# Other ranks and times in the list that orders a fused attention, Fourier mixing and feed-forward kernel

## The chip, the core and the metric

One core of a Trainium2 chip runs the whole program. It has a matrix engine (TensorE, PE), three engines for elementwise work (VectorE or DVE, ScalarE or ACT, GpSimd or POOL) and a synchronising engine (SyncE, SP), which issues most transfers. Each engine executes its own list of instructions in order, and waits on semaphores for the others. The metric is the device time of one execution in microseconds; the lower the better.

## What is computed

Attention with a causal window over 8 batches, 8 heads and 576 positions of 64 features (half of the heads look at every fourth position), then a layer that mixes tokens by the real part of a two-dimensional Fourier transform, normalises, and applies a feed-forward product with 512 by 2048 by 512 weights. All in float32; the weights come as 64-bit floats, which the kernel converts on the chip.

```
scores = where(mask, q @ k.T / 8, -1e9); attn = softmax(scores); x = attn @ v    # (8, 576, 512)
u  = x + real(fft(fft(x, axis=1), axis=2))
un = (u - mean(u)) / sqrt(var(u) + 1e-6)
out = u + relu(un @ w_ch1) @ w_ch2
```

## The kernel before

**An order by rank.** No instruction is written in its final place. Every step is entered with `add(engine, cost, fn, reads, writes, prio)`; then `Plan.run` walks through an imagined time with the entered costs. Whenever an engine is free, it takes of the steps whose inputs are ready the one with the smallest `prio`. The order that comes out is the program's; each engine then runs it in order on the chip, whatever the true durations are. So a number in the table of ranks (`P_...`) can move instructions all over the program.

**Early stage, to about 600 us.** For each batch b, `attention(b)` works on 4 pairs of heads, each in three units of two blocks: score products (L581, bank `sc`), a masked maximum on VectorE (L589, it needs `mask_sb`), exponentials on ScalarE (L595), transposes on TensorE (L608), products with the values (L615) and a normalisation (L627); results go to DRAM. `mix(b)` reads them, folds them (L760), transforms along the sequence (L797) and the channels (L843), and normalises. The 2048 hidden features are 16 blocks of 128. Six of them are *resident*: `prep_w` converts their 64-bit weights once (L922 to L941, twelve conversions into `wa1` and `wa2`). `fill(ut, tiles)` runs these six blocks for two tiles of 128 tokens: `up` (L1021, 72 matmuls per two tiles, corrected on VectorE at L1029) and then `down` (L1037, 36 matmuls, the second products), and `keep_part` stores the two part sums.

**Handover.** Meanwhile `blocks` converts the other ten blocks (tile `wst`, stored in DRAM as `wt`). When the transform is done, `left_w` takes its place in SBUF; when the conversions are done, `late_w` takes the staging buffers' place, and the last weights go into the seats of the resident ones (`places`).

**Late stage.** Ten hidden blocks are five pairs, worked off for nine chunks of 512 tokens by a scheme of seven block products in place of eight. `load_blocks(c)` reads a chunk's rows (L1132, four transfers), transposes them on VectorE (L1142), forms four differences (L1192) and fills `xb` (casts at L1202, corrections at L1205). `two_tiles(p)` issues seven up products (L1351, all into one PSUM bank, `ff`, in groups of 6 or 12 matmuls); after each group `snap` copies the bank out on ScalarE (L1359) before the next one may write it; sums and operands follow on VectorE (L1387, L1376, L1380). `down7` issues the second products (L1459). `prepare` fetches the tokens' rows and part sums, `finish` writes the output. The ranks here are `SOON + 0.001 * clock` for elementwise work and `LAST + 0.01 * clock` for matmuls, where `clock` counts the second products issued so far; up products are ahead by `P_UP`.

## Time and profile before

| | |
|---|---|
| median of 3 runs | 1074.49 us (1071.9 to 1077.31) |
| profiled execution | 1072.93 us, span 1071.2 us |
| TensorE busy / its weight loads | 1031.3 us (96%) / 964.0 us (90%) |
| VectorE busy | 888.1 us (83%) |
| ScalarE busy | 623.9 us (58%) |
| GpSimd busy | 221.0 us (21%) |
| moved by transfers | 158.19 MB, 148 GB/s over the span |
| chain that ended last | PE 77%, DVE 12%, DMA 6% |

Busy shares are averages over stages with different limits. Ends of matmuls are modelled, so the busy time of TensorE is no measure of its peak. The granted clock tells which of TensorE's two levels holds: 1.00 is 2.4 GHz, 0.50 is 1.2 GHz. The profiled execution is 1.56 us below the median of the three runs, and 1.7 us longer than its span.

### The profile page before, as it was taken

What the parts mean: (1) busy time and instruction counts of PE and PEld (TensorE: products, weight loads), DVE (VectorE), ACT (ScalarE), POOL (GpSimd) and SP (SyncE); (2) the same over time, 40 slices, a digit from 0 to 9 for tenths busy, and PEclk for the clock granted to TensorE, in tenths of its full rate; (3) what the DMA queues carried; (4) which work ended last, traced back from release to release, by engine and by line L of the source; (5) the groups of instructions that cost most, each with busy time, mean ns of one, the idle gap of its engine ahead of it and who ended that gap; (6) DMA issues with size and microseconds to landing.
All of it is one profiled execution on the core that took longest, in us unless ns stands there. A gap on an engine that the chain in (4) does not pass through costs nothing.

```text
span 1071.2 us, 22723 instructions
## 1 busy us (share of the span) xinstructions
PE 1031.3 (96%) x7876; PEld 964.0 (90%) x7876; DVE 888.1 (83%) x2847; ACT 623.9 (58%) x1588; POOL 221.0 (21%) x278
## 2 busy tenths in 40 slices
PE   4899999999999999999999899999999999999996
PEld 3778898888899899999899799999999999999996
DVE  4898996987888956669988568989998989989886
ACT  3798775865745232345445356666665757565753
POOL 1021524364463545400000000201010000110020
PEclk9899999999999999999999899999999999999999
DMA  8968855865545325254778952333323242332131
GB/s 271 284 208 260 241 167 160 228 200 161 181 126 161 95 86 147 69 168 138 238 254 255 332 199 40 99 63 106 82 87 85 76 110 66 102 80 89 31 103 57
DMA packets 116451, 158.19 MB, mean 148 GB/s; under 512 B 11032, under 2 KB 64472, under 8 KB 116336
## 3 DMA queue, kind: packets, MB, share of 16 engines
q1 hardware_dynamic: 112752, 148.03, 47.5%
q0 software_dynamic: 3040, 8.09, 2.5%
q8 instruction: 62, 1.02, 0.4%
q10 hardware_dynamic: 544, 0.62, 0.2%
q14 instruction: 53, 0.43, 0.1%
HBM read 108.40 MB, written 48.29 MB: 146 GB/s over the span
## 4 chain that ended last, share of the span: by engine, by line
PE 77%; DVE 12%; DMA 6%; issue 2%; ACT 1%; SPq 1%; DVEq 0%; ACTq 0%
PE ff L1351 19%; PE ff L1021 9%; PE ff L1037 8%; PE sc L581 7%; PE sc L1459 5%; PE mix L1459 5%; PE av L615 4%; PE mix L843 3%; PE pt L1459 3%; PE av L1459 3%; PE ff L1459 3%; PE mix L797 2%; DMA ut<-us 2%; PE pt L608 2%; DVE ut L1142 2%
## 5 line engine op out<-in xcount | busy, mean ns | idle before, releaser
L595 ACT ACTIVATE pm<-pm,mx 96x128 f32<-96x128 f32 x384 | 129.2, 394 | 37.2 <-DVE mx L589 35.3
L1076 POOL DMA_INDIRECT ut<-us,flip_sb x20 | 36.3, 1816 | 536.2 <-DMA wa<-wt 132.0
L1021 PE MATMUL ff<-ut,wa 128*128 128x256 f32 x936 | 125.6, 285 | 2.4 <-DVE h L1029 2.4
L581 PE MATMUL sc<-kb,tq 128*96 128x256 f32 x384 | 109.6, 403 | 15.1 <-issue 9.9
L1021 PEld LDWEIGHTS ff<-ut,wa 128*128 128x128 f32 x936 | 116.4, 188 | 4.6 <-DVE h L1029 2.8
L589 DVE CUSTOM_DVE_ANT_0 pm<-sc,mask_sb 96x128 f32<-96x128 f32 x384 | 91.6, 279 | 26.9 <-DMA mask_sb<-in_mask_dram 9.3
L1037 PE MATMUL ff<-wa,h 128*128 128x512 f32 x468 | 113.9, 394 | 0.0
L1037 PEld LDWEIGHTS ff<-wa,h 128*128 128x128 f32 x468 | 85.9, 188 | 16.6
L1142 DVE STREAM_TRANSPOSE ut<-ut 128x512 f32<-128x512 f32 (+1 forms) x76 | 73.0, 988 | 14.4 <-DMA ut<-us 14.2
L581 PEld LDWEIGHTS sc<-kb,tq 128*96 128x96 f32 x384 | 57.6, 173 | 29.2 <-issue 15.5
L615 PEld LDWEIGHTS av<-vt,ptsb 128*96 128x96 f32 x672 | 68.8, 167 | 12.1 <-DVE xt L627 3.2
L1351 PE MATMUL ff<-xb,wa 128*128 128x256 f32 x540 | 76.4, 281 | 0.8 <-ACT s L1359 0.6
L615 PE MATMUL av<-vt,ptsb 128*96 128x65 f32 x672 | 71.9, 249 | 5.3 <-DVE xt L627 4.1
L1351 PEld LDWEIGHTS ff<-xb,wa 128*128 128x128 f32 x540 | 68.4, 188 | 2.2 <-ACT s L1359 1.0
L1351 PE MATMUL ff<-xb,left_w 128*128 128x256 f32 x486 | 68.1, 281 | 0.8 <-ACT s L1359 0.5
L1351 PE MATMUL ff<-xb,late_w 128*128 128x256 f32 x486 | 68.3, 279 | 0.0
L1373 ACT ACTIVATE h<-s 128x256 fp32r<-128x256 f32 x136 | 55.1, 415 | 13.7 <-DVE s L1389 8.9
L1351 PEld LDWEIGHTS ff<-xb,left_w 128*128 128x128 f32 x486 | 61.7, 188 | 1.5 <-ACT s L1359 0.9
L1351 PEld LDWEIGHTS ff<-xb,late_w 128*128 128x128 f32 x486 | 61.8, 188 | 0.4 <-ACT ut L1359 0.2
L1027 ACT ACTIVATE h<-ff 128x256 fp32r<-128x256 f32 x78 | 30.0, 384 | 54.2 <-PE ff L1021 53.8
L1351 PE MATMUL ff<-xb,right_w 128*128 128x256 f32 x378 | 53.4, 286 | 5.1 <-ACT ut L1359 3.2
L1029 DVE SCALAR_TENSOR_TENSOR h<-ff,h 128x256 fp32r<-128x256 f32 x78 | 32.6, 418 | 26.5 <-ACT h L1027 25.9
(247 smaller groups left out, 2593.0 us busy)
## 6 DMA issues: line engine op xcount, KB each, us to landing
vt<-in_v_dram SPq DMA_DIRECT2D x32, 390.0 KB
wst<-in_w_dram SPq DMA_DIRECT2D x20, 512.0 KB
wt<-wst SPq DMA_DIRECT2D x40, 256.0 KB
us<-uc SPq DMA_DIRECT2D x36, 257.0 KB
part<-row SPq DMA_DIRECT2D x36, 256.0 KB
ut<-us SPq DMA_DIRECT2D x36, 256.0 KB
ut<-part SPq DMA_DIRECT2D x36, 256.0 KB
kb<-in_k_dram SPq DMA_DIRECT2D x62, 144.0 KB
```

The lines of the kernel that those rows point to most:

```text
L581: nc.tensor.matmul(sc()[:QB, 256 * n:256 * n + 256], lhsT=tq()[:, cols], rhs=kb()[:, :, keys], start=True, stop=True,)
L589: nc.vector.tensor_tensor_reduce(pm()[:, i], sc()[:QB, KB * i:KB * i + KB], mask_sb()[:, masks[blocks[i // 2]]], -0.125, 3.0e38, ALU.add, ...
L595: add("ACT", 0.295, lambda i=i: nc.scalar.activation(out=pm()[:, i], in_=pm()[:, i], func=AF.Exp, bias=mx()[:, i:i + 1], scale=-1.0), ((mx ...
L615: add("PE", 0.17, lambda i=i: nc.tensor.matmul(av()[:QB, 65 * i:65 * i + 65], lhsT=pt()[:, i], rhs=vt()[:, i % 2, blocks[i // 2]], start=T ...
L1021: nc.tensor.matmul(z()[:, :n_tok], lhsT=wf()[:, a, kk], rhs=ut()[:, p, kk], start=(kk == 0 and n == 0), stop=(kk == KT - 1 and n == 2),)
L1029: add("DVE", dve(n_tok), lambda: nc.vector.scalar_tensor_tensor(h()[:, 1, :n_tok], z()[:, :n_tok], 0.0, h()[:, 0, :n_tok].bitcast(F32), op ...
L1037: nc.tensor.matmul(acc(), lhsT=h()[:, a, P * s:P * s + P], rhs=wf()[:, p], start=(first and n == 0), stop=(last and n == 2),)
L1076: add("POOL", 1.3, lambda: nc.gpsimd.indirect_dma_start(u(0, C + 2), None, us[idx // 4](), bass.IndirectOffsetOnAxis(ap=flip_sb()[:, 4 * k ...
L1142: nc.vector.transpose(out=o[back], in_=x[:, g])
L1351: nc.tensor.matmul(up_bank()[:, lo:lo + TOK1], lhsT=ap()[:, a, kk], rhs=xb()[:, j, p, kk], start=(start and k == 0), stop=(k == 5), skip_g ...
L1373: add("ACT", act(TOK1), lambda: nc.scalar.activation(out=ap()[:, 0], in_=src(), func=AF.Relu if relu else AF.Copy), need, (k0,), prio)
L1459: nc.tensor.matmul(acc()[:, TOK1 * half:TOK1 * half + TOK1], lhsT=ap()[:, a, P * half:P * half + P], rhs=wap()[:, q_].rearrange("p k f -> ...
```

## The change

It does four things. *Ranks*: the table of priorities has other numbers for attention, folds, fills, late loads and preparations; up products get `P_UP` 10.35 in place of 0.2, which ranks them ahead of all second products; small additions per batch and per conversion (`P_WS`, `P_MS`, `P_SS`) are new. *Last fill*: the second products of the last two resident tiles get their own rank, `LAST + P_BR`, and alternate between two banks. *Second chunk*: its rows and the preparations of the first chunk wait for a mark, which is set when the first pair's last operand is there. *First transfers*: mask, identity and permutation tables and the first values get ranks of -7 to -7.9, and the first queries and keys -7.8 in place of -25.06. Seats of the last weights go to all of `wa1` first, then to `wa2`. Some assumed costs of transfers on SP changed too.

```diff
-P_OP, P_GA, P_LB, P_FI = 0.0, 53.71, -74.28, 47.3
-P_PR = 91.31
-P_UP = 0.2
+P_OP, P_GA, P_LB, P_FI = 2.43, 48.72, -40.68, 47.3
+P_PR = 128.43
+P_UP = 10.35
+P_WS = [10, 11, 11, 10, 10, 10]
+P_SS = [10, 10, 10, 10, 15, 12, 10, 10]
+P_BR = -0.125
+LB_AT, PR_AT = 0, 0
...
-P_QK0, P_V0 = -25.06, -7.0
+P_QK0, P_V0 = -7.8, -7.0
...
-T_SEQ, T_CHN, T_STEP, P_SEQ, P_CHN = 7.07, 23.47, 3.91, -21.94, -1.92
+T_SEQ, T_CHN, T_STEP, P_SEQ, P_CHN = 10.36, 24.62, 1.0, -4.0, -2.0
...
-P_MASK, P_ID, P_PERM = -7.35, -14.41, 8.87
+P_MASK, P_ID, P_PERM = -7.9, -7.8, -7.0
...
-    def prepare(idx, seat, prio):
+    def prepare(idx, seat, prio, mark):
...
+        add("NONE", 0.0, lambda: None, (marks[mark],) if mark[0] == 0 else (), (uk,), prio)
...
-        add("NONE", 0.0, lambda: raw(), (), (raw,), prio)
+        add("NONE", 0.0, lambda: raw(), (marks[0, LB_AT],) if c == 1 else (), (raw,), prio)
...
+        if tiles[-1] == NTILE - 1:
+            accs = [bank("sc") for _ in tiles]
+            for f in range(NF1):
+                for s, acc in enumerate(accs):
+                    down(hs[f], wa2[f], acc, s, f == 0, f == NF1 - 1, LAST + P_BR)
+            for idx, acc in zip(tiles, accs):
+                keep_part(idx, acc, prio)
+            return
...
-        prep_w(f, wa1[f], wa2[f], utb, (), P_W + P_WF * f)
+        prep_w(f, wa1[f], wa2[f], utb, (), P_W + P_WF * f + P_WS[f] - 10)
...
-    places += [(x, i) for f in range(NF1) for x in (wa1[f], wa2[f]) for i in range(2)]
+    places += [(x, i) for wa in (wa1, wa2) for x in wa for i in range(2)]
...
             got = two_tiles(p)
+            marks[c, p] = Buf(ap=0)
+            add("NONE", 0.0, lambda: None, got[2][0], (marks[c, p],), SOON)
```

How the order moves is shown at three places. Line numbers of the changed file are higher, by 5 up to the resident fills, by 14 in the late stage. First, SP's list from the first transfers of the program, as far as the first values (`vt`). Before, from the second pair's keys on (the first pair's keys and queries stand ahead):

```order
L553 DMA kb1_175<-in_k_dram 64x576 x2
L556 DMA tq_255<-in_q_dram 128x576
L553 DMA kb2_176<-in_k_dram 64x576 x2
L556 DMA tq_266<-in_q_dram 128x576
L493 DMA ident_sb_163<-in_ident_dram 128x384
L492 DMA mask_sb_162<-in_mask_dram 96x384
L558 DMA vt_275<-in_v_dram 128x780
```

In the changed program the list begins with the mask (the queries and keys of the first pair come in thirds):

```order
L497 DMA mask_sb_162<-in_mask_dram 96x384
L498 DMA ident_sb_163<-in_ident_dram 128x384
L561 DMA tq_230<-in_q_dram 128x192
L558 DMA kb0_174<-in_k_dram 64x192 x2
L561 DMA tq_230<-in_q_dram 128x192
L558 DMA kb0_174<-in_k_dram 64x192 x2
L561 DMA tq_230<-in_q_dram 128x192
L499 DMA perm_sb_164<-in_perm_dram 96x288
L563 DMA vt_260<-in_v_dram 128x780
L558 DMA kb1_175<-in_k_dram 64x576 x2
```

The mask moved from behind all three pairs' queries and keys to the front, and the first values from behind them to between the first and the second pair. Second, TensorE's list at the handover; `ut` holds the last tiles' tokens, `h` their hidden values, `xb` the first late chunk. Before:

```order
L1037 MATMUL sc_8664<-wa2_2_158,h_8574 128x512 x3
L1037 MATMUL sc_8664<-wa2_3_159,h_8598 128x512 x3
L1037 MATMUL sc_8664<-wa2_4_160,h_8617 128x512 x3
L1037 MATMUL sc_8664<-wa2_5_161,h_8648 128x512 x3
L1351 MATMUL ff_8692<-xb_7169,right_w_5404 128x256 x36
L1459 MATMUL sc_8761<-right_w_5404,h_8743 128x256 x6
L1351 MATMUL ff_8692<-xb_7169,right_w_5404 128x256 x6
L1459 MATMUL av_8789<-left_w_7167,h_8779 128x256 x4
```

In the changed program:

```order
L1026 MATMUL av_8612<-ut_8252,wa1_5_155 128x256 x12
L1365 MATMUL ff_8638<-xb_7153,right_w_5449 128x256 x6
L1042 MATMUL sc_8649<-wa2_0_156,h_8526 128x512 x3
L1042 MATMUL sc_8587<-wa2_1_157,h_8544 128x512 x3
L1365 MATMUL ff_8638<-xb_7153,right_w_5449 128x256 x12
L1042 MATMUL sc_8649<-wa2_1_157,h_8544 128x512 x3
L1042 MATMUL sc_8587<-wa2_2_158,h_8573 128x512 x3
L1365 MATMUL ff_8638<-xb_7153,right_w_5449 128x256 x12
L1042 MATMUL sc_8649<-wa2_2_158,h_8573 128x512 x3
L1042 MATMUL sc_8587<-wa2_3_159,h_8592 128x512 x3
L1365 MATMUL ff_8638<-xb_7153,right_w_5449 128x256 x6
```

The first 36 matmuls of the up products stood in a row behind all second products of the last fill; now they begin directly behind its up products, and six second products stand between each two groups. Third, VectorE's list at the same place, from the correction of the fill's last hidden block (L1029, L1034). Before:

```order
L1029 SCALAR_TENSOR_TENSOR h<-av,h 128x256
L1142 STREAM_TRANSPOSE ut<-ut 128x4x4x32 x4
L1192 TENSOR_TENSOR ut<-ut 128x512 x3
L1387 TENSOR_TENSOR ut<-ut,ys 128x256
L1192 TENSOR_TENSOR ut<-ut 128x512
L1082 SCALAR_TENSOR_TENSOR ut<-ut 128x512
L1376 SCALAR_TENSOR_TENSOR h<-ut,h 128x256
```

In the changed program:

```order
L1034 SCALAR_TENSOR_TENSOR h<-av,h 128x256
L1401 TENSOR_TENSOR ut<-ut,ys 128x256
L1390 SCALAR_TENSOR_TENSOR h<-ut,h 128x256
L1401 TENSOR_TENSOR sb<-sb 128x256
L1403 SCALAR_TENSOR_TENSOR sb<-ut,sb 128x256
L1401 TENSOR_TENSOR s_8728<-s_8728,ut 128x256
```

The second chunk's transposes and differences are gone from here; the first of the transposes follows 31 rows behind the first sum.

## Rows read from the trace of the kernel before

**Rows 1.** Busy time by stage: us of PE, PEld, DVE, ACT, POOL; clock; DMA share; GB/s.

```profile
core 0: us, PE busy (x) PEld busy (x) DVE busy (x) ACT busy (x) POOL busy (x), PEclk, DMA share, GB/s
0.00:25.00 25.00, 11.12 (x47) 7.72 (x48) 9.79 (x73) 7.12 (x20) 3.52 (x10) 1.00 0.89 272
25.00:150.00 125.00, 117.95 (x906) 100.44 (x905) 115.72 (x633) 100.92 (x292) 33.82 (x46) 0.96 0.79 236
150.00:350.00 200.00, 197.41 (x1503) 176.39 (x1502) 163.21 (x766) 121.65 (x341) 91.87 (x127) 1.00 0.61 173
350.00:595.00 245.00, 243.91 (x1612) 223.80 (x1613) 192.95 (x452) 102.36 (x248) 55.49 (x76) 1.00 0.54 167
595.00:625.00 30.00, 24.91 (x157) 22.82 (x156) 16.53 (x32) 12.46 (x28) 2.04 (x2) 0.89 1.08 346
625.00:1050.00 425.00, 423.43 (x3557) 420.52 (x3556) 375.65 (x864) 273.96 (x649) 34.30 (x18) 1.00 0.31 82
```

**Rows 2.** Timeline of the start, all engines: start us, us, instruction, idle before it.

```profile
3.73 3.70 PE L581 MATMUL sc<-kb,tq 128*96 128x256 f32 x8 [3.73 <-DMA kb<-in_k_dram]
...
6.77 0.09 DVE L506 MEMSET kb<- 64x32 f32 x1
...
8.87 0.43 SPq L492 DMA_DIRECT2D mask_sb<-in_mask_dram  x1
...
16.30 0.29 DVE L589 CUSTOM_DVE_ANT_0 pm<-sc,mask_sb 96x128 f32<-96x128 f32 x1 [9.32 <-DMA mask_sb<-in_mask_dram]
...
17.34 5.18 PE L581 MATMUL sc<-kb,tq 128*96 128x256 f32 x12 [9.91 <-issue]
```

**Rows 3.** Busy time in three short windows of the early stage, columns as in rows 1.

```profile
10.00:15.00 5.00, 0.00 (x0) 0.00 (x0) 0.00 (x0) 0.00 (x0) 0.15 (x1) 1.00 1.13 368
...
40.00:45.00 5.00, 2.63 (x13) 2.08 (x13) 4.90 (x11) 3.06 (x8) 0.00 (x0) 0.76 0.81 244
45.00:50.00 5.00, 4.66 (x23) 3.87 (x23) 4.49 (x20) 1.31 (x3) 0.00 (x0) 0.50 0.83 237
```

**Rows 4.** Groups of VectorE's instructions by line, 0 to 160 us: busy us, mean ns.

```profile
L934 DVE SCALAR_TENSOR_TENSOR ut<-ut 128x512 f32<-128x512 f32 x12 | 8.8, 731 | 0.1
L941 DVE TENSOR_TENSOR wa<-ut,wa 128x512 fp32r<-128x512 f32 x12 | 8.5, 707 | 0.3 <-ACT wa L940 0.3
L928 DVE SCALAR_TENSOR_TENSOR ut<-ut 128x512 uint32<-128x512 uint32 x12 | 8.2, 687 | 0.0
L931 DVE SCALAR_TENSOR_TENSOR ut<-ut 128x512 uint32<-128x512 uint32 x12 | 8.2, 679 | 0.0
...
L925 DVE TENSOR_SCALAR ut<-ut 128x512 uint32<-128x512 uint32 x12 | 5.2, 434 | 0.0
```

**Rows 5.** Timeline of TensorE at the handover to the late stage.

```profile
595.32 7.00 PE L1037 MATMUL sc<-wa,h 128*128 128x512 f32 x30
602.15 0.87 PE L1351 MATMUL ff<-xb,right_w 128*128 128x256 f32 x6
603.48 1.65 PE L1351 MATMUL ff<-xb,right_w 128*128 128x256 f32 x12 [0.46 <-ACT ys L1359]
608.38 2.24 PE L1351 MATMUL ff<-xb,right_w 128*128 128x256 f32 x12 [3.25 <-ACT ut L1359]
612.00 1.65 PE L1351 MATMUL ff<-xb,right_w 128*128 128x256 f32 x6 [1.39 <-ACT sb L1359]
```

**Rows 6.** Timeline of VectorE at the handover to the late stage.

```profile
593.21 0.68 DVE L1205 TENSOR_TENSOR xb<-ut,xb 128x512 fp32r<-128x512 f32 x1
...
604.76 4.00 DVE L1142 STREAM_TRANSPOSE ut<-ut 128x512 f32<-128x512 f32 x4 [8.34 <-DMA ut<-us]
...
610.61 0.41 DVE L1387 TENSOR_TENSOR ut<-ut,ys 128x256 f32<-128x256 f32 x1
```

**Rows 7.** Chain of waits at the handover, in order of time: start us, us, what.

```profile
594.44 10.23 DMA ut<-us
```

**Rows 8.** Timeline of TensorE, the first resident fill.

```profile
126.30 0.94 PE L1021 MATMUL ff<-ut,wa 128*128 128x256 f32 x6
```

More of the change, by code (lines that the diff above doesn't have):

```diff
@@ L921, in words_of @@
         src = ((t, "src"),)
-        dma(lambda: nc.sync.dma_start(out=shaped(flat(0, 2 * C, I64)), in_=rows), gate, src, prio + P_WD, P * 4096)
+        dma(lambda: nc.sync.dma_start(out=shaped(flat(0, 2 * C, I64)), in_=rows), gate, src, prio + P_WD, P * 4096, 0.63)
         add("ACT", 0.57, lambda: nc.scalar.activation(
@@ L1172, in fused_kernel @@
     xb = Buf()
-    spare, later = {}, []
+    spare, later, marks = {}, [], {}
     late_w = Buf()
```

23 lines of the change are left out of this document (12 added, 11 removed).

## The prediction

> **What bounds the kernel now.** I read the windows by stage first [rows 1]. From 625 to 1050 us TensorE is busy 423.43 of 425 us and its weight loads 420.52, at full clock: the late stage is bound by TensorE and has 1.6 us of visible idle time to give. From 350 to 595 it is busy 243.91 of 245. Idle TensorE time stands in two places. In the first 25 us it is busy 11.12, and VectorE only 9.79, while from 25 to 150 us VectorE is busy 115.72 of 125 and TensorE 117.95: the early stage is held by VectorE, with TensorE close behind. And from 595 to 625 TensorE is busy 24.91 of 30 at a mean clock of 0.89, between two stretches in which it never rests. So I looked at these two places line by line.
>
> At the start [rows 2] the first eight scores run at 3.73 us, VectorE has done its clearing by 6.86, and then it sits until 16.30 for one transfer, the mask, which SP issues at 8.87, after all of the first queries and keys. TensorE waits with it (9.91 us before the row at 17.34), because both score banks are full. In the handover from the resident fills to the late stage [rows 5, 6, 7] the last 30 second products of the fills end at about 602.15, the first late up product follows, and then TensorE stands 0.46, 3.25 and 1.39 us. The wait is not for data of its own chunk: VectorE's queue holds the four transposes of the second chunk (604.76, after 8.34 us of idling for the rows' transfer of 10.23 us) and then three of its differences ahead of the sum at 610.61 that the first chunk's second operand needs. The chain of waits runs through exactly these rows.
>
> **The change, part by part.** *Handover, removed stalls.* The idle time is 0.46 + 3.25 + 1.39 = 5.1 us, which is also 30 - 24.91 of the stage [rows 1, 5]. The clock fell from 2.4 to 1.2 GHz after that idling: a mean of 0.89 over 30 us is 6.6 us at half speed, in which 3.3 us of work is lost; 1.4 us of it overlaps the last idle piece, which takes 0.7 off. Together 5.1 + 2.6 = 7.7 us. In the new order VectorE's queue has the first chunk's sums directly behind the last fills, and the second chunk's transposes 31 rows later; on TensorE each of the first groups of up products is followed by six second products of the last fill. One of these takes 6.83 / 30 = 0.228 us [rows 5], so six cover 1.37 us, against 0.46 us of bare wait for the copy out of the single up bank [rows 5]. All 36 make 8.2 us, work that was done anyhow. I put the remaining stall at nothing; without that cover it would be about 0.46 us at each of four to five groups, 2 us.
>
> *Handover, what comes late instead.* The second chunk's rows (four transfers on SP) now go behind the forty weight transfers and two result rows. They take 10.23 us [rows 7], their transposes 4 us and the differences some 2 us [rows 6]; the chunk is wanted only when the first is through, and the late stage's nine chunks take about 450 / 9 = 50 us each, so some 30 us are left over: nothing. The blocks that go into the second half of the resident weights' seats wait for the fill's second products, 8 us later than now, and are wanted in the last pair, some 40 us on: nothing. The two tiles' part rows leave later by the same 8 us; they are read only when the mark of the first pair has passed: nothing.
>
> *Start.* The mask and the identity now go out first on SP, and the values of the first head pairs ahead of the second and third pair's keys. Bounds of what it brings: the wait itself is 9.32 us [rows 2], and VectorE can't start before 6.86, when its clearing ends, which is what is left if the first scores land by then. They landed at 3.73; 336 KB (144 and 192 by their shapes) now go ahead of the queries. At the 272 GB/s of the first 25 us [rows 1] this is an estimated 1.2 us, so they still land before 6.86. If VectorE then worked as densely as from 25 to 150 us, the first stage would win more: it idles 25 - 9.79 = 15.2 us of the first 25, and at 7% idle, as from 25 to 150, it would idle 1.9, so at most 13.3 us. The low end is nothing: from 10 to 15 us the DMA engines moved 368 GB/s at a share of 1.13 [rows 3], so they were not waiting for anybody, and what was fetched meanwhile (keys, values, tables, weights) has to be fetched in any order. I take 8.0, the wait less the time that the first values need to arrive, because VectorE is the engine that binds up to 150 us [rows 1], and an idle engine that binds is time lost.
>
> Here a rule stands against the change. The Trainium skill, "DMA: Bandwidth & Descriptors", section "Issuing engines are not separate DMA queues", says that transfers from all issuing engines run on the same 16 DMA engines and interleave. By that rule a transfer put first only makes the others later, and the front's gain would be nothing; the trace agrees as far as the full share at 10 to 15 us goes, and it is the second rival below.
>
> *Conversion of the resident weights.* The twelve conversions cost VectorE 5.2 + 8.2 + 8.2 + 8.8 + 8.5 = 38.9 us [rows 4]. In the order before, six of them are ahead of the first fold of the sequence transform, now one; nine are ahead of the first resident hidden block's correction in both orders. So they are moved behind attention, not saved. The first resident fill (126.30 us now [rows 8]) stands behind 120 score products on TensorE, where it stood behind 94. That gives attention more of VectorE early, and costs nothing as long as attention feeds TensorE meanwhile. Where the conversions piled up in the order before, it did not: from 40 to 45 us VectorE is busy 4.90 and TensorE 2.63 of 5, and the clock went to its lower level up to 50 us [rows 3].
>
> *The rest of the order.* From 150 to 595 us everything shifts by small amounts, since the priorities of folds, fills and weights all changed. TensorE idles 2.6 us from 150 to 350 and 1.1 from 350 to 595 [rows 1], so at most 3.7 us can be won; a loss is bounded by nothing but a new wait, for which the order shows no place. The late stage's up products are now ranked ahead of every waiting second product; the order alternates groups of up products with seven or eight second products, now without exception from the second chunk on but for one place in the last. At most 1.6 us. For both I take zero, with -3 to +3 in the range.
>
> **Sum.** The profiled execution took 1072.93 us (span 1071.2). 1072.93 - 7.7 - 8.0 = 1057.2. The median of the three runs is 1.56 above the profiled one, so for a median 1058.8, say 1059.
>
> **Rivals.** *The front's gain is lost on the way* (chance 0.27). Either the DMA engines set the pace of the first 40 us, or the first late chunk doesn't get ready sooner. For the second: its last piece is ready at 593.9 [rows 6], 1.4 us before the fill's second products begin at 595.3. The wait for it was covered by 6.8 us of these products, and now the first up product stands ahead of them in TensorE's queue. If the chain of late weights and tokens on VectorE keeps its time while the fills end 8 us sooner, TensorE waits those 8 us there. Against: that chain starts when the transform of the last batch ends, which is on TensorE's list too and moves with it. It would give 1074.5 - 7.7 = 1067.
>
> *A denser front* (0.15). The bound of 13.3 us is reached and the late stage gives its 1.6: 1074.5 - 7.7 - 13.3 - 1.6 = 1052. For it: VectorE, ScalarE and TensorE would be loaded almost alike in the new order up to the first fill.
>
> *The new rank doesn't act* (0.06). The first chunk is late for another reason, the 36 products are stuck behind the up product, the handover costs what it did and only the start is won: 1074.5 - 8.0 = 1066.5.
>
> *Slower* (0.05). The conversions, now late, come between TensorE and its first fills: VectorE converts while attention stands still, and TensorE has nothing, as at 40 to 45 us. If all 38.9 us were uncovered, the time would be 1074.5 + 38.9 - 15.7 = 1098; it is slower than before from 15.7 us uncovered on, two fifths of them. Against: in VectorE's new list the longest stretch without a mask contains the corrections of the first fills, so TensorE has these fills there.
>
> **How the numbers follow.** The forecast has 0.47, the rivals 0.27, 0.15, 0.06 and 0.05. A difference under 0.5%, 5.4 us, is about what a measurement of this kernel can't tell from none; faster means under 1069.1. The forecast, the dense front, most of the two rivals at 1067 are under it, together 0.87; 0.08 is for a front rival that also loses some us in the reordered middle; 0.05 slower. The range reaches from 1050 (dense front, and 3 us in the middle) to 1069 (front lost, and 2 us of the middle's bound).
>
> **What would show it.** Right: VectorE's first mask before 8 us; a first 25 us with VectorE busy 19 or more; no TensorE wait over 0.5 us between the last fills and the second pair, and no lower clock there; the first late up product at about 587 (595 less 8). Wrong: a wait of TensorE for a cast of the first chunk with 36 second products still queued; keys or values as releasers of early scores; a low clock or conversions without TensorE work before the first fill; new waits at chunk boundaries, above all for the second chunk. The transfer of the rows, if it came to lie on the path again, would cost its 10 us.

## The result, and the profile after

The changed kernel takes 1078.47 us (median of 20 runs, 1074.85 to 1083.78), the kernel before 1072.68 in 20 runs beside it: a ratio of 1.0052 [1.0038, 1.0065], 5.8 us slower. The prediction was 1059. The profiled execution of the changed kernel took 1077.81 us, with a span of 1076.0.

The windows by stage, columns as in [rows 1], the second stage in four pieces:

```profile
0.00:25.00 25.00, 18.81 (x125) 14.02 (x125) 17.43 (x119) 15.00 (x42) 3.08 (x9) 1.00 0.93 263
25.00:50.00 25.00, 22.92 (x140) 17.53 (x140) 15.09 (x107) 16.16 (x48) 2.67 (x5) 0.86 0.88 256
50.00:75.00 25.00, 24.01 (x190) 20.20 (x191) 21.77 (x138) 21.75 (x64) 8.26 (x12) 1.00 0.84 256
75.00:100.00 25.00, 24.70 (x197) 21.27 (x196) 23.38 (x131) 21.29 (x64) 5.91 (x8) 1.00 0.87 255
100.00:150.00 50.00, 42.46 (x312) 34.43 (x311) 48.20 (x263) 40.04 (x114) 19.09 (x23) 0.97 0.91 257
150.00:350.00 200.00, 197.41 (x1507) 177.95 (x1505) 164.50 (x719) 117.53 (x325) 88.30 (x126) 1.00 0.56 162
350.00:595.00 245.00, 241.08 (x1575) 220.74 (x1576) 193.78 (x451) 101.16 (x247) 56.24 (x76) 0.99 0.53 162
595.00:625.00 30.00, 23.19 (x158) 21.57 (x157) 10.04 (x24) 9.12 (x22) 2.04 (x2) 0.91 1.03 374
```

In the first 25 us VectorE is busy 17.43 us where it was 9.79 [rows 1]: the start did become denser, by 7.6 us. But from 25 to 50 us it is busy 15.09, where 23.83 stood before, and summed to 150 us it is 125.87 after and 125.51 before (the first five rows, and 9.79 + 115.72): on VectorE the gain has been given back. Two stretches of before, for comparison:

```profile
25.00:50.00 25.00, 21.89 (x155) 18.08 (x154) 23.83 (x118) 18.75 (x52) 2.42 (x5) 0.85 0.94 276
100.00:150.00 50.00, 47.84 (x385) 42.32 (x384) 48.82 (x254) 38.93 (x111) 22.68 (x29) 1.00 0.72 210
```

The handover, 595 to 625, has TensorE busy 23.19 of 30, less than the 24.91 of [rows 1].

The start, line by line: VectorE's first masked maximum, and a piece of the timeline of all engines from 33 to 37 us.

```profile
6.89 0.29 DVE L594 CUSTOM_DVE_ANT_0 pm<-sc,mask_sb 96x128 f32<-96x128 f32 x1
```

```profile
33.22 0.59 PE L613 MATMUL mix<-perm_sb,pm 96*128 96x96 f32 x2 [0.65 <-ACT pm L600]
...
36.63 0.29 DVE L594 CUSTOM_DVE_ANT_0 pm<-sc,mask_sb 96x128 f32<-96x128 f32 x1 [3.35 <-PE sc L586]
...
36.96 1.28 ACT L600 ACTIVATE pm<-pm,mx 96x128 f32<-96x128 f32 x4 [2.63 <-DVE mx L594]
```

The 9.32 us wait for the mask [rows 2] is gone. In its place the three engines wait for one another in turn: VectorE for scores, ScalarE for VectorE's maximum, TensorE for ScalarE's exponentials.

The handover on TensorE, which answers to [rows 5]:

```profile
597.94 0.87 PE L1365 MATMUL ff<-xb,right_w 128*128 128x256 f32 x6
598.65 1.54 PE L1042 MATMUL sc<-wa,h 128*128 128x512 f32 x6
600.03 1.59 PE L1365 MATMUL ff<-xb,right_w 128*128 128x256 f32 x12
...
616.23 0.40 PE L1473 MATMUL sc<-left_w,h 128*128 128x256 f32 x2
623.44 1.65 PE L1365 MATMUL ff<-xb,left_w 128*128 128x256 f32 x6 [6.81 <-ACT sb L1373]
```

Up products and the fill's second products alternate without a wait until 616.6, as forecast; then there is one wait of 6.81 us, longer than the three of before together (5.1). Who holds ScalarE shows on its own timeline, and SP's list shows why:

```profile
622.50 0.42 ACT L1387 ACTIVATE row<-s 128x256 fp32r<-128x256 f32 x1 [8.57 <-DMA part<-row]
```

```profile
597.42 11.74 SPq L1014 DMA_DIRECT2D late_w<-wt  x16
609.56 7.44 SPq L1014 DMA_DIRECT2D wa<-wt  x12
617.30 0.32 SPq L1061 DMA_DIRECT2D part<-row  x1
...
621.18 2.65 SPq L1138 DMA_DIRECT2D ut<-us  x4
```

The tiles `row`, into which the last fill's part sums are copied, serve again as seats of late operands (L1387 writes one at 622.50). So that operand waits until the part sum has been stored, and the store is issued at 617.30, behind 28 weight transfers in SP's list. The chain of waits, which ran through the rows' transfer before [rows 7], now reads:

```profile
612.25 4.99 DMA wa<-wt
...
617.30 5.11 DMA part<-row
...
622.50 0.42 ACT row L1387
622.91 0.48 ACT sb L1373
...
623.44 1.65 PE ff L1365 x6
```

To place the losses I use one more reading. For each matmul started after a time *t* of a profiled execution I count its duration at full clock (0.1178 us with 256 columns, 0.228 with 512, from the spacing of rows that don't wait), and add the sum to *t*. If TensorE never stood still behind *t*, this figure would not move; its rise between two times is the time lost there, by waiting or at the lower clock. "End" is the start of the last matmul. It is one profiled execution each, which may lie some 4 us off its kernel's median (tables_only 4.0 below, after_late 4.2 above), so a difference counts only where it recurs.

```
              at 590   lost 590-640   lost 640-680   lost 680-end   end
before        1047.3        8.6            1.2            5.2       1062.3
after         1050.4       10.2            1.0            5.6       1067.3
hand_only     1048.3        8.5            1.1            9.4       1067.3
front_only    1049.7       10.7            0.8            7.8       1069.0
after_store   1050.2        8.7            2.5            6.8       1068.2
hand_rows     1046.9       11.1            0.2            9.1       1067.3
hand_late     1048.2        0.4           10.1            9.0       1067.7
hand_mid      1047.5        0.4            7.5            9.0       1064.5
keep_rows     1046.5        0.9            1.4            6.6       1055.3
mask_light    1041.9        9.1            1.2            5.4       1057.6
light_rows    1041.5        0.9            1.6            6.5       1050.5
```

Of the 5.0 us between before and after, 3.1 are there by 590 us and 1.6 come in the handover.

### The profile page after: what moved, and what is told of

It reads as the page before. It is cut to its first block, busy times and chain, and to the rows that moved or that the text cites. A ratio compares the mean times of both kernels' runs of the same rounds, so it can differ in the third digit from the quotient of the medians.

```text
span 1076.0 us, 22711 instructions
## 1 busy us (share of the span) xinstructions
PE 1035.3 (96%) x7876; PEld 965.3 (90%) x7876; DVE 893.0 (83%) x2847; ACT 623.9 (58%) x1588; POOL 211.4 (20%) x278
## 4 chain that ended last, share of the span: by engine, by line
PE 58%; DVE 11%; DMA 5%; ACT 1%; issue 1%; SPq 0%; POOL 0%; DVEq 0%; ACTq 0%
PE ff L1365 16%; PE ff L1026 7%; PE ff L1042 7%; PE mix L1473 5%; PE sc L1473 5%; PE pt L1473 2%; PE ff L1473 2%; PE sc L1042 2%; PE av L1473 2%; PE mix L848 2%; PE av L1026 1%; PE pt L1026 1%; PE mix L802 1%; DMA late_w<-wt 1%; PE sc L586 1%
## 5 line engine op out<-in xcount | busy, mean ns | idle before, releaser
L1082 POOL DMA_INDIRECT ut<-us,flip_sb x20 | 27.9, 1395 | 543.2 <-ACT h L1387 181.0
L1387 ACT ACTIVATE h<-s 128x256 fp32r<-128x256 f32 x136 | 55.4, 415 | 16.8 <-DVE s L1403 8.5
L1060 ACT COPY row<-ff 128x512 f32<-128x512 f32 x26 | 15.2, 586 | 65.1 <-PE ff L1042 53.1
L1034 DVE SCALAR_TENSOR_TENSOR h<-ff,h 128x256 fp32r<-128x256 f32 x78 | 32.7, 419 | 23.1 <-ACT h L1032 22.7
```

What stands on the lines that cost most here:

```text
L1034: add("DVE", dve(n_tok), lambda: nc.vector.scalar_tensor_tensor(h()[:, 1, :n_tok], z()[:, :n_tok], 0.0, h()[:, 0, :n_tok].bitcast(F32), op ...
L1387: add("ACT", act(TOK1), lambda: nc.scalar.activation(out=ap()[:, 0], in_=src(), func=AF.Relu if relu else AF.Copy), need, (k0,), prio)
```

## The experiments

Times are medians, in brackets the kernel before, run beside it, then the ratio with its interval. Line numbers differ by a few from kernel to kernel.

### Which half costs the time?

**hand_only**: before with the handover's part of the change (late ranks, last fill, marks, seats) and before's early ranks. **front_only**: before with the early ranks and the planner's entered costs of the change, and before's handover.

```diff
+P_OP, P_GA, P_LB, P_FI = 2.43, 48.72, -40.68, 47.3
+P_PR = 128.43
+P_UP = 10.35
...
+        if tiles[-1] == NTILE - 1:
+            accs = [bank("sc") for _ in tiles]
...
+            marks[c, p] = Buf(ap=0)
```

```diff
-P_QK0, P_V0 = -25.06, -7.0
+P_QK0, P_V0 = -7.8, -7.0
...
-P_MASK, P_ID, P_PERM = -7.35, -14.41, 8.87
+P_MASK, P_ID, P_PERM = -7.9, -7.8, -7.0
```

> The kernel before with the handover half of the change alone: the mark that holds back the second chunk's rows and the first preparations, the own rank and the two banks of the last fill's second products, the late ranks and the seats. Everything up to the last fill keeps the order of before. Theory A (the gain of the handover is eaten there by a new wait: operands go into the two row tiles, which still wait for their part sums to be stored): the old stall of 5.1 us is gone, a new one of 6 to 7 us stands some 25 us later, the time is 1075 us, 2 above before. Theory B (the handover brings its 7.7 us, and the changed kernel loses only in the early stage): 1065 us.

> The kernel before with the early half of the change alone: first transfers, ranks of attention, folds, fills and conversions, assumed costs of transfers. The late ranks, the last fill and the second chunk are those of before. Theory A (the early gain of 13 us is lost again by 330 us and 4 us more between 345 and 600 us): 1075 to 1076 us, the last fill begins 2 to 3 us later than before. Theory B (the early half is the whole loss, the handover brought 7.7): 1086 us. Theory C (the early half gains and only the handover loses): under 1069 us.

hand_only 1077.76 [1072.32], 1.0053 [1.0034, 1.0072]; front_only 1077.13, 1.0050 [1.0030, 1.0071]. Each half alone makes the kernel slower. hand_only has the new wait of TensorE (5.27 us before 620.83) and loses as much from 590 to 640 as before did, 8.5 against 8.6: the wait takes back all that the alternation won. front_only is 2.4 us late by 590 us; it has a second wait in the middle fills that before has not:

```profile
351.65 4.51 PE L1024 MATMUL ff<-ut,wa 128*128 128x256 f32 x36 [2.23 <-DVE h L1032]
369.73 2.49 PE L1024 MATMUL ff<-ut,wa 128*128 128x256 f32 x14 [1.84 <-DVE h L1032]
```

The same reading, with the other shapes of the early stage counted by their own spacing (0.082 to 0.215 us), tells where the early half loses. The first two rows are means: of the seven kernels here with before's early ranks (before, hand_only, hand_store, hand_rows, hand_late, hand_mid, keep_rows), and of the five with the change's (after, front_only, after_store, after_rows, after_late). The last two are one execution each; both kernels are described below.

```
                      lost 0-100  100-150  150-350  350-400  400-590   at 590
before's early ranks     31.6        4.5      7.1      1.0      0.7    1047.3
change's early ranks     21.1       13.6      7.6      5.6      0.1    1050.4
mask_first               32.2        4.2      7.1      3.8      0.7    1050.4
after_conv               32.8        6.9      7.2      5.3      0.4    1054.9
```

From 0 to 100, 100 to 150 and 350 to 400 us the two groups don't overlap (350 to 400: 0.4 to 1.9 against 4.8 to 6.0). So the changed early order leads by 10.5 us at 100 us, gives 9.1 back by 150, and loses another 4.6 from 350 to 400. The lead is borrowed: by 50 us VectorE has done 2.5 us of the conversions of the resident weights in after, 12.5 in before; from 100 to 150 us it does 18.1 for 11.7, and TensorE waits for VectorE's other work between them. From 350 to 400 TensorE waits twice for VectorE's corrections, and 36 up products behind the first wait take 5.99 us where 36 x 0.118 = 4.2 is full speed: the granted clock is 0.83 from 350 to 360 us. Three rows of after:

```profile
126.42 0.86 PE L620 MATMUL av<-vt,ptsb 128*96 128x65 f32 x8 [0.87 <-DVE xt L632]
129.86 0.86 PE L620 MATMUL av<-vt,ptsb 128*96 128x65 f32 x8 [1.25 <-DVE xt L632]
...
352.25 5.99 PE L1026 MATMUL ff<-ut,wa 128*128 128x256 f32 x36 [2.63 <-DVE h L1034]
```

Which of the early ranks brings the waits from 350 to 400 us was not separated.

The halves don't add up (5.4 and 4.8, together 5.8). By the table hand_only loses 4 us more than before and after behind 680 us; all kernels made of before's early half with the change's late ranks do (9.0 to 9.4). There it is spread over waits of a few tenths of a microsecond, and whether the ranks or the order that the plan makes of them cause it was not separated; front_only loses 7.8 there without these ranks.

### What holds the handover?

**after_store** and **hand_store** issue the two part stores from ScalarE's queue, directly behind the copies, in after and in hand_only. A new field `behind` emits a step behind its partner while the plan keeps its order, so every other instruction stands where it stood.

```diff
-        dma(lambda: nc.sync.dma_start(out=parts[idx](), in_=row()), (row,), (parts[idx],), prio, P * 2048 * ROW)
+        last = idx >= NTILE - 2
+        stored = dma(lambda: (nc.scalar if last else nc.sync).dma_start(out=parts[idx](), in_=row()),
+                     (row,), (parts[idx],), prio, P * 2048 * ROW)
+        if last:
+            stored.behind = copied
```

> The changed kernel with one thing different: the last fill's two part sums are stored from ScalarE's queue, each directly behind the copy that makes it, in place of SP's queue, where they stand behind 28 weight transfers. All other instructions of TensorE, VectorE, ScalarE and GpSimd keep their order. Theory A (the 6.8 us stall is these stores): ScalarE's wait of 8.6 us falls to about 2 us (a store takes some 5 us and the row is wanted 3.3 us after its copy), TensorE's stall to 0.5 to 2 us, the low clock behind it goes too: 1070 to 1073 us. Rival (the stall is the transfers' bandwidth, whoever issues): within 2 us of the changed kernel, 1077 to 1078.

> Handover half alone, and the last fill's two part sums stored from ScalarE's queue directly behind their copies. Theory A: as the changed kernel gains by it, 6 to 8 us below the handover half alone: 1067 to 1069 us, below the kernel before. Rival (bandwidth): 1075 us. If theory B of the first run holds: 1065 us, as without it.

after_store 1079.71 [1072.32], 1.0066 [1.0046, 1.0086]; hand_store 1077.12, 1.0044 [1.0028, 1.0061]. The cause named was right and its removal brought nothing. ScalarE's timeline and then TensorE's and VectorE's, in after_store:

```profile
610.50 0.36 ACTq L1069 DMA_DIRECT2D part<-row  x1
...
615.27 0.42 ACT L1398 ACTIVATE row<-s 128x256 fp32r<-128x256 f32 x1 [0.97 <-DMA part<-row]
```

```profile
637.03 1.65 PE L1376 MATMUL ff<-xb,late_w 128*128 128x256 f32 x6 [6.11 <-ACT ys L1384]
```

```profile
633.94 1.08 DVE L1159 STREAM_TRANSPOSE ut<-ut 128x512 f32<-128x512 f32 x1 [7.47 <-DMA ut<-us]
```

The wait at 616 is gone, and some 14 us later there is the next, 6.11 us: VectorE's list has the second chunk's transposes ahead of the first chunk's sums, and their rows were issued at 621.98, again behind all weights. This is the stall of [rows 6], one pair later.

**hand_rows** and **after_rows** take that away too: the rows are fetched early, only the transposes wait for the mark (added to hand_store and after_store).

```diff
-        add("NONE", 0.0, lambda: raw(), (marks[0, LB_AT],) if c == 1 else (), (raw,), prio)
+        add("NONE", 0.0, lambda: raw(), (), (raw,), prio)
+        if c == 1:
+            add("NONE", 0.0, lambda: tr(), (marks[0, LB_AT],), (tr,), prio)
```

> The handover half alone, the last fill's part sums stored from ScalarE's queue, and of the second chunk only the transposes held back to the mark: its rows are fetched as early as before, ahead of the weights in SP's queue. Theory (what eats the handover's gain is always something queued on SP behind 28 to 32 weight transfers of 0.74 us: first the part sums, without them the second chunk's rows): no stall of TensorE over 1 us from 595 to 660 us, the last fill's end and the first chunk as dense as with the change, and 5 us less than hand_store, of which 2 to 3 go to small waits of the new order in the late stage: 1067 to 1070 us. Rival (weights themselves come too late, so TensorE waits in the third to fifth pair): a stall of some us at a late or resident weight seat, 1072 to 1076.

> The changed kernel with the same two repairs (part sums stored from ScalarE's queue; the second chunk's rows fetched early, only their transposes held back). Theory: it loses only what the early half costs, so 2 to 3 us over hand_rows, 1070 to 1073 us, 5 to 8 less than the changed kernel. Rival (the handover is not what costs the changed kernel): 1076 or more.

hand_rows 1078.43 [1073.55], 1.0043 [1.0027, 1.0059]; after_rows 1081.02, 1.0066 [1.0050, 1.0082]. A third holder of the same kind comes up. SP's list, ScalarE and TensorE of hand_rows:

```profile
614.49 9.80 SPq L1018 DMA_DIRECT2D wa<-wt  x14
624.58 0.91 SPq L1087 DMA_DIRECT2D ut<-us  x2
```

```profile
629.65 0.72 ACT L1093 ACTIVATE ut<-ut 128x512 f32<-128x512 f32 x1 [8.42 <-DMA ut<-us]
```

```profile
631.20 2.93 PE L1375 MATMUL ff<-xb,late_w 128*128 128x256 f32 x12 [7.54 <-ACT ut L1383]
```

Now it is the tokens' rows for the first chunk's preparation, which ScalarE's list wants (L1093) ahead of the copies out of the up bank.

**hand_late**, **after_late** and **hand_mid** hold everything back: rows, and the preparations entered with the fourth pair behind the third pair's mark (late), or with the third pair behind the second's (mid); stores on ScalarE's queue. First the edit of hand_late and after_late, then what hand_mid has in its place:

```diff
-LB_AT, PR_AT = 0, 0
+LB_AT, PR_AT = 2, 2
...
-            if p == 1:
+            if p == (1 if c else 3):
```

```diff
-LB_AT, PR_AT = 2, 2
+LB_AT, PR_AT = 1, 1
...
-            if p == (1 if c else 3):
+            if p == (1 if c else 2):
```

> The handover half alone, with everything that stood behind the weight transfers on SP taken out of the way: the last fill's part sums are stored from ScalarE's queue, the second chunk's rows wait for the third pair's mark, and the first chunk's preparations are entered two pairs later and wait for the same mark. Theory (the stall that moved three times is one thing: what waits in SP's queue for 40 weight transfers at some 400 GB/s; with nothing wanted before they are through at 625 us, TensorE doesn't stop): no wait of TensorE over 1 us from 590 to 650 us, the 420th late up product at 698 to 700 us in place of 705, the end at 1069 to 1072 us. Rival (the order of the late ranks costs more than the handover brings): no stall, but 1073 us or more. Second rival (the weights themselves are late, since the transfers set the pace of this stretch too): a stall of 3 us or more at a weight of the fourth or fifth pair.

> The changed kernel with the same repairs. Theory: 5 to 8 us under the changed kernel, 1071 to 1073; what is left over the kernel before is the early half. Rival (the transfers set the pace of the handover): 1076 or more, with a stall at a late weight.

> As hand_late, but held back less: the second chunk's rows wait for the second pair's mark, and the first chunk's preparations are entered with the third pair and wait for the same mark. Theory A (the handover's gain is real, and hand_late gave it back at the first chunk boundary because what was held back fell there onto VectorE, which is busy 39 of 40 us from 640 to 680): no stall from 595 to 640 us, VectorE busier from 630 to 645 and TensorE's wait at 649 us under 1 us; 1068 to 1072 us, 6 or more under hand_late. Theory B (the work that the second chunk and the preparations bring doesn't fit beside the first chunk in any place): 1075 or more, with the loss somewhere between 620 and 700 us.

hand_late 1078.67 [1072.58], 1.0051 [1.0033, 1.0070]; after_late 1082.86, 1.0087 [1.0073, 1.0102]; hand_mid 1076.22 [1073.07], 1.0032 [1.0018, 1.0046]. The handover itself is now clean, and the loss stands at the end of the first chunk (in after_late also behind 680 us, 15.1 us, for a cause that stays open). Windows of hand_mid:

```profile
595.00:625.00 30.00, 29.79 (x221) 28.20 (x221) 13.06 (x32) 14.23 (x33) 2.03 (x2) 1.00 1.05 350
625.00:655.00 30.00, 30.00 (x258) 30.00 (x258) 26.44 (x58) 21.94 (x51) 0.00 (x0) 1.00 0.35 70
655.00:685.00 30.00, 26.23 (x194) 24.55 (x193) 27.60 (x60) 12.96 (x32) 2.01 (x2) 0.94 0.36 99
```

TensorE is busy 29.79 and 30.00 of 30, then 26.23: what was held back now stands in VectorE's list just when the second chunk is wanted. VectorE's load alone doesn't explain the loss: from 655 to 685 us it is busy 27.60 of 30 here, 27.09 in before and 28.89 in keep_rows, where TensorE is busy 29.54 and 29.72; that the order is what costs the time is argued, not shown. By the table the handover loses 0.4 us in place of 8.6, and 640 to 680 loses 7.5 in place of 1.2.

**keep_rows** spreads it, and leaves the change's late ranks out: before with its own late ranks and seats, the last fill in two banks, the stores on ScalarE's queue, rows fetched early with only the transposes held to the first pair's mark, and only the preparations held far back.

```diff
+LB_AT, PR_AT = 0, 2
+P_BR = -0.125
...
+        if c == 1:
+            add("NONE", 0.0, lambda: tr(), (marks[0, LB_AT],), (tr,), prio)
...
-            if p == 1:
+            if p == (1 if c else 3):
```

> The kernel before with its own late ranks and seats, and of the handover only: the last fill's second products between the first up products and in two banks, its part sums stored from ScalarE's queue, the second chunk's rows fetched as early as before with only their transposes held to the first pair's mark, and the first chunk's preparations entered with the fourth pair behind the third pair's mark. Theory A (the handover is worth its 7.7 us if what is held back is spread over the first chunk, and the late ranks of the change cost 2 to 3 us of their own from 800 us on): no stall over 1 us from 595 to 650 us, at most 3 us lost around the first chunk boundary, 1065 to 1068 us. Theory B (whatever is moved, the first two chunks give it back): 1072 us or more.

keep_rows 1067.06 [1073.37], 0.9940 [0.9920, 0.9960]: 6.3 us faster than before. Its handover:

```profile
595.00:625.00 30.00, 29.38 (x218) 27.82 (x217) 18.52 (x40) 13.12 (x32) 1.88 (x2) 1.00 0.99 310
```

TensorE 29.38 of 30 at full clock; the table has 0.9 us lost from 590 to 640 where before had 8.6, and hardly more than before from 640 to 680. Against hand_rows, keep_rows differs in two things, the late ranks with the seats and the preparations held far back; which of them frees the end was not separated.

### What holds the start?

**mask_first**: before with the same order on every engine, only four transfers stand earlier in SP's list (the recorded expectations count six): mask and identity first, the first two pairs' values behind their queries. **mask_rows**: the same on hand_rows.

```diff
-        dma(lambda: nc.sync.dma_start(out=mask_sb(), in_=mask), (), (mask_sb,), P_MASK, QB * 3 * KB * 4)
+        dma(lambda: nc.sync.dma_start(out=mask_sb(), in_=mask), (), (mask_sb,), P_MASK, QB * 3 * KB * 4).behind = "start"
...
+        if b == 0 and dil == 0:
+            values.behind = asked
```

> The kernel before, with the order of every engine kept, in which only six transfers on SP are issued earlier: mask and identity ahead of all, the first two pairs' values directly behind their queries. Theory A (VectorE's wait of 9.3 us for the mask is time lost, and the early half of the change lost the gain by its new order alone): VectorE's first mask before 8 us, everything behind it some 8 us earlier up to the first fill (118 in place of 126 us), 1064 to 1066 us. Theory B (the transfers set the pace of the first 40 us): keys, values or weights become the next releasers, and 0 to 3 us are left, 1070 to 1073. Theory C (the gain gets as far as the middle and is lost there, since VectorE's or ScalarE's work up to 330 us holds TensorE): first fill 8 us earlier, last fill as before.

> hand_rows and mask_first together: the handover half with both repairs, and the six early transfers. If the two gains are independent, the sum of both: 1059 to 1064 us under theory A of mask_first, 1066 to 1070 under B or C. Rival: the start's gain runs into a chunk that isn't ready, and the handover takes it back: as hand_rows.

mask_first 1074.35 [1073.55], 1.0007 [0.9994, 1.0020]: no change. mask_rows 1079.90, 1.0059 [1.0042, 1.0076]: no gain over hand_rows either. Windows of mask_first:

```profile
10.00:20.00 10.00, 7.43 (x32) 6.03 (x33) 2.87 (x26) 4.09 (x14) 1.53 (x4) 0.59 1.18 337
20.00:30.00 10.00, 7.62 (x45) 6.30 (x44) 5.24 (x26) 4.62 (x12) 1.29 (x3) 0.67 1.19 325
```

The mask is early, the first product with values starts at 17.5 us in place of 23.4, and then the engines wait again, TensorE 3.27 us before 12.57 for a transfer, VectorE 3.51 us before 24.68 for the weights: the DMA engines are full (1.18, 1.19), and the 48th score product comes at 39.1 us, not before the 38.1 of the old order. By 50 us VectorE has done 33.10 us of work, before 33.63. In this stretch a transfer put first made others late. The Trainium skill ("DMA: Bandwidth & Descriptors", section "Issuing engines are not separate DMA queues") says that transfers of all issuing engines run on the same 16 DMA engines and interleave; the trace agrees, with shares of 1.18 and 1.19.

**mask_light** and **tables_only** take bytes away: the ten transform tables (2.8 MB: four of 290 KB, four of 258, one of 435, one of 129), which GpSimd fetched beside the first keys, go behind the seventh normalisation, in mask_first and in before. **after_light** does it in after.

```diff
+        if (b, dil, j, u) == (0, 1, 0, 0):
+            for x in touches:
+                x.behind = normal
```

> The kernel before with the six earlier transfers (as mask_first), and the ten tables of the transform (2.9 MB of the 10 MB that move in the first 35 us) fetched only behind the seventh normalisation, at 30 to 40 us, in place of 7 to 28 us. All other instructions keep their order. Theory A (the transfers set the pace of the first 40 us, so an earlier mask only changes who waits): with fewer bytes ahead of it the first stage runs 4 to 8 us sooner, the 48th score at 32 to 35 us in place of 39; as far as nothing gives it back, 1066 to 1070 us. Theory B (latencies between the engines set the pace, not bytes): 38 to 39 us for the 48th score, and 1072 to 1075 us. If the tables come too late for the first transform at 79 us, the time is above before.

> The kernel before with the late tables alone; mask, identity and values are issued where they were. Theory A (it is the bytes ahead that count, not which transfer goes first): most of the gain of mask_light without its six transfers, the 48th score at 33 to 35 us, 1068 to 1070 us. Theory B (both are needed: early mask to start, fewer bytes to go on): the 48th score at 36 us or later, 1071 to 1073 us.

> The changed kernel with the ten tables of the transform fetched only behind the seventh normalisation (25 to 40 us); everything else keeps its order. Theory A (in the changed kernel too, bytes set the pace of the first 40 us, and that is where its start was lost): VectorE busier than 15.1 us from 25 to 50 us, the 48th score before 30 us in place of 32.0, first fill some 4 us sooner, and 3 to 6 us less in all: 1072 to 1075. Theory B (the loss of 25 to 50 us is the new order's own, with too few scores ahead): 31 to 32 us for the 48th score, 1077 to 1079.

mask_light 1067.49 [1072.58], 0.9952 [0.9938, 0.9966]; tables_only 1071.22 [1073.07], 0.9984 [0.9972, 0.9996]; after_light 1079.28 [1073.07], 1.0051 [1.0035, 1.0067]. Windows of mask_light, and one of after_light:

```profile
20.00:30.00 10.00, 9.72 (x86) 8.64 (x87) 9.52 (x60) 9.63 (x28) 0.00 (x0) 1.00 0.96 275
30.00:40.00 10.00, 7.64 (x46) 5.83 (x44) 9.89 (x46) 7.15 (x19) 2.60 (x5) 0.85 0.83 238
```

```profile
20.00:30.00 10.00, 9.44 (x67) 6.69 (x66) 6.57 (x56) 7.42 (x23) 0.00 (x0) 1.00 0.71 189
```

In before's order bytes set the pace: with the tables out of the way VectorE is 9.52 of 10 busy from 20 us on, the 48th score comes at 31.9 us, and the kernel is 5.1 us faster. The mask's place then counts: 5.1 us with it, 1.9 without. In the changed order the DMA share falls to 0.71 and VectorE stays at 6.57 of 10: there the engines wait for one another, as in the rows from 33 us on, and not for bytes. after_light is no faster than after.

**after_conv**: after with the conversions of the resident weights ranked early again.

```diff
-P_QK, P_V, P_TR, P_MIX, P_SPAN, P_W, P_WF, P_FILL, P_FILLT = -8.0, -5.24, -5.0, 4.32, 9.95, 30, 9.45, 42.52, 12.2
+P_QK, P_V, P_TR, P_MIX, P_SPAN, P_W, P_WF, P_FILL, P_FILLT = -8.0, -5.24, -5.0, 4.32, 9.95, 8, 9.45, 42.52, 12.2
```

> The changed kernel with one number different: the rank of the first conversion, 8 in place of 30, so that the twelve conversions of the resident weights are spread over attention nearly as in the kernel before (the fifth to eighth end behind 112 to 152 masked maxima; 88 to 156 before, 196 to 228 with the change), and the first resident fill stands behind 98 score products (94, 120). Theory A (pushing the conversions behind attention leaves TensorE without cover from 100 to 155 us, where it is busy 42 of 50 and less): TensorE busy 46 or more from 100 to 150 us, the first fill before 135 us, and 3 to 5 us less than the changed kernel. Theory B (the early stage is bound by what VectorE and the transfers have to do in all, whatever the order): the first fill earlier, but the last one within 1.5 us of the changed kernel, and the time too.

after_conv 1089.84 [1072.58], 1.0162 [1.0139, 1.0186]. Both expectations missed. TensorE is denser where after is thin, but thinner just ahead of it:

```profile
75.00:100.00 25.00, 22.82 (x146) 18.77 (x147) 20.45 (x93) 17.55 (x48) 6.63 (x6) 0.86 0.79 224
100.00:150.00 50.00, 45.85 (x359) 39.49 (x358) 48.41 (x247) 38.70 (x108) 23.10 (x30) 1.00 0.79 226
```

The first fill comes at 137.5 us (after 152.3, before 126.3), yet the last fill's up products end at 602.7, in after at 598.1, and the wait at the handover is 7.26 us. One number moves the whole list. By the early table the loss moves with the conversions: 6.9 us from 100 to 150 where the changed order has 13.6, but 32.8 before 100 us where it has 21.1. Done early, they cost the lead; done late, they take it back. The 350 to 400 us loss stays (5.3).

### Do the gains add up?

**light_mid**: hand_mid and mask_light together. **light_rows**: keep_rows and mask_light together. Both get the edits of mask_light:

```diff
+        dma(lambda: nc.sync.dma_start(out=mask_sb(), in_=mask), (), (mask_sb,), P_MASK, QB * 3 * KB * 4).behind = "start"
...
+        if (b, dil, j, u) == (0, 1, 0, 0):
+            for x in touches:
+                x.behind = normal
```

> hand_mid with the six early transfers and the late tables of mask_light. If the start and the handover are independent, 5 us under hand_mid: 1063 to 1067 us under its theory A, 1070 under B.

> keep_rows with the six early transfers and the late tables of mask_light. If the start and the handover are independent: 5 us under keep_rows, 1060 to 1063 us under its theory A and 1067 under B.

light_mid 1069.41 [1073.07], 0.9959 [0.9945, 0.9972]; light_rows 1061.82 [1073.37], 0.9895 [0.9875, 0.9916]. They add up: 6.3 and 5.1 make 11.4, and light_rows is 11.6 us faster than before. It beats both kernels.

## Why the prediction was wrong, by its own steps

**What bounds the kernel** was read rightly for the kernel before: the two places, the start and the handover, hold what light_rows then won, 11.6 of the 15.7 us predicted, the start's share of it by fewer bytes and not by the change's order. What the prediction did not have is that the new order loses time in two places of its own, from 100 to 150 and from 350 to 400 us.

**Handover, removed stalls (-7.7).** The mechanism holds: the three waits of [rows 5] are gone, the clock is kept, six second products cover each copy, and keep_rows loses 8.6 - 0.9 = 7.7 us less from 590 to 640, 6.3 by medians. That 7.7 comes out to the tenth is luck, with one execution of each. In the changed kernel the term measured +1.6, in hand_only -0.1, since the next step failed.

**Handover, what comes late instead (nothing).** This step failed, three times over. "The two tiles' part rows leave later ... nothing" looked for the readers of the rows in DRAM and not for the next writer of the tile that they leave: a late operand, 6.81 us. "Some 30 us are left over" for the second chunk's rows reckoned when the chunk is wanted and not when VectorE's in-order list reaches its transposes: behind the second row stands the first chunk's own work (6.11 us in after_store). The preparations' rows, not named at all, are the third (7.54 us in hand_rows). The prediction itself said that the rows stand behind forty weight transfers; it priced the transfer and not the place in the list. [rows 1] had the price: from 595 to 625 us the DMA engines are full (1.08) at 346 GB/s, at which 28 weights of 256 KB (7.3 MB) take 21 us; issued from 597.4 on they put the store at 618.6, and it went at 617.30. The planner errs the same way: it enters 0.52 us for a weight's transfer, and after's list issues 16 in 11.74 us, 0.73 each, so everything behind 28 of them would come some 6 us (28 x 0.21, an estimate) later than planned.

**Start (-8.0).** A lead of about this size was there, 10.5 us at 100 us, but not for the reason given, and none of it reached the end. Putting the mask first wins nothing by itself: mask_first is at +0.8 us, interval about zero. Its low bound, "nothing: ... what was fetched meanwhile has to be fetched in any order", was the right end for before's order; the row that decided was [rows 3], a DMA share of 1.13 while every engine idled. I chose the high end because VectorE binds up to 150 us, but a binding engine's idle time is won only if its inputs can come sooner, and VectorE's busy time by 50 us is 32.52 after (17.43 + 15.09) and 33.63 before. The lead on TensorE came from conversions put off, so that its size is near 8.0 is luck. In the changed order a second limit stands behind the bytes, the round trip between the engines, which no row of before could show. The rival "the front's gain is lost on the way" (the first one; the prediction's remark on the 16 DMA engines calls it the second) had the bytes in its first half, at 1067; what it lacked was the handover.

**Conversion of the resident weights (nothing).** This step failed too. The condition, "as long as attention feeds TensorE", did not hold: TensorE is busy 42.46 of 50 us from 100 to 150, where before had 47.84, the first fill comes 26 us later, and 13.6 us are lost in place of 4.5. That they are "moved behind attention, not saved" was right; the price of the move, put at nothing, was 9.1 us and took back nearly all of the start's lead.

**The rest of the order (0, within 3).** This failed by its bound. From 150 to 350 us it holds (7.6 us lost for 7.1). From 350 to 400 the changed early order loses 4.6 us more, by two waits (2.63 and 1.67 us in after, where before has one of 1.97) and the lower clock behind one of them, though "the order shows no place" for a new wait. The place is sensitive in before's order too: mask_first loses 3.8 there in its one execution. The late stage's up products, priced at zero: after loses 5.6 us behind 680 us, before 5.2, which is right for after (with before's early half it was 9.0 to 9.4, see hand_only).

**The rivals and the chances.** "Slower" had one mechanism, uncovered conversions, and 0.05. It came in part, 9.1 of the 15.7 us that it needed, enough to use up the start. The other mechanism, a store or a row at the end of SP's list on which an in-order engine stands, was mentioned only in the last sentence of the prediction and had no chance of its own. Of the signs, the first mask before 8 us came (6.89); VectorE was busy 17.43 in the first 25 us and not 19, and the first late up product came at 597.94 and not at about 587.

## What to carry to other kernels

A wait for one transfer while the DMA engines are full need not be lost time that a new order can win: take bytes out of that stretch first (the tables, 1.9 us), then put the wanted transfer ahead (with it, 5.1 us). A lead at one place can be borrowed from work put off; look where that work comes due before counting the lead as won. Where a transfer is held back, follow its tile's next writer and every in-order list that names its result, at the measured pace of the list it is queued in; when one holder is removed, look for the next before calling the stall solved.

## What the runs showed that was not expected

The two part stores take about as long from either queue: 5.11 us from SP (617.30 in after), 4.8 us from ScalarE's (610.50 to 615.27 in after_store), while SP issues 32 weight transfers between 597.00 and 621.34. What stood in the way was the turn to be issued, 6.7 us from the end of the copy (610.60) to the issue. The Trainium skill ("DMA: Bandwidth & Descriptors", section "Issuing engines are not separate DMA queues") says that issuing from another engine saves only the sequencer's time, usually small relative to the transfer; here the saved turn was longer than the transfer, and the measurement decides.

One wait costs more than itself: behind TensorE's 7.54 us in hand_rows the granted clock is 0.50, the lower level, from 631 to 636 us, and 12 up products take 2.93 us (after has 1.59 at 600.03). The window with the end of the wait in it (columns as above):

```profile
625.00:640.00 15.00, 8.80 (x51) 8.52 (x52) 5.75 (x14) 6.53 (x15) 0.00 (x0) 0.66 0.41 153
```
